# A spectral-mixer backward kernel: gelu products in the loaded tile, symmetric matrices without transposes, and gradient rows through a ring of three tiles

## Chip, cores, metric

One core of one Trainium2 chip. The metric is device time in microseconds (us) of one execution. Every run quoted here was in the fast state (granted TensorE clock 0.96 to 0.99 over the span); a trace is of one of these executions.

## The reference

A block with adaptive layer norm: a spectral filter (`rfft2`, product with a complex weight, `irfft2`), then an MLP with gelu. The kernel returns the output and all gradients, in bfloat16.

```python
# S = 2048 tokens, D = 1024, F = 3584
mod = (silu(c) @ w_mod).reshape(1, 6, 1, D)          # sa, ca, ga, sb, cb, gb
h = layernorm(x) * (1 + ca) + sa
x = x + ga * irfft2(rfft2(h) * (w_r + 1j * w_i))
h = layernorm(x) * (1 + cb) + sb
x = x + gb * (gelu(layernorm(h) @ w1 + b1) @ w2 + b2)
# outputs: x and the vjp for x, w_r, w_i, w1, b1, w2, b2, c, w_mod
```

## The kernel before

The transforms are products with cosine and sine matrices on TensorE. Three pieces of the program matter here; the cuts leave out hints to the scheduler.

(`tt` is a VectorE operation on two tensors.) The gelu block. The MLP runs over 28 of these (4 token blocks of 512, 7 groups of 512 features). Working tiles come in two sets, so block n+2 writes the tiles of block n. `ph` holds a product computed earlier (the gradient that comes back through w2), and `d_gz` takes the gradient that later stages read.

```python
zb, av, bv, sg, ph = gts[n % 2]
nc.sync.dma_start(out=ph, in_=d_ph_v[...])
for k in range(4):
    ...                                   # 8 matmuls into a bank pz
    nc.scalar.activation(out=zb[:, k, :], in_=pz[:], func=ACT.Identity, bias=...)   # evacuation, L767
nc.scalar.activation(out=av, in_=zb, func=ACT.Square)                               # L769
nc.vector.tensor_scalar(out=av, ...)
tt(bv, av, zb, ALU.mult)
nc.scalar.activation(out=sg, in_=bv, func=ACT.Sigmoid, ...)                         # L773
nc.scalar.activation(out=bv, in_=bv, func=ACT.Sigmoid, ...)
...                                       # more of the gelu on VectorE, result in av
for k in range(4):
    nc.vector.tensor_tensor_reduce(out=av[:, k, :], in0=ph[:, k, :], in1=av[:, k, :], ...)   # L784
nc.gpsimd.dma_start(out=d_gz_v[...], in_=av)                                        # L786
```

The spectral core, which runs forward and backward. It walks over eight pairs of frequency blocks; on the way it loads matrices transposed for the inverse transform.

```python
def load_smi(par):                        # par 0: even, par 1: odd matrices
    for t in range(2):
        for i in range(4):
            nc.sync.dma_start_transpose(out=smi[:, t, :, i * P:(i + 1) * P], in_=d_SF[:, par + 2 * t, i, :])
...
if par == 0 and m == 2:
    for cl in range(4):
        for h in range(2):
            nc.sync.dma_start_transpose(out=gm[...], in_=d_E[:, 0 if fwd else 1, 2 * cl + h, :])
```

The rows of the modulation weight's gradient, done beside the backward pairs: one step loads a tile of `w_mod`, scales the gradient row into an output tile, stores that, and reduces. There is one output tile (`gmy[:, 1:2]`) and one loaded tile.

```python
def gmod_steps(r, wrs, gws, gr):
    ...                                   # load the gradient row gr; wr, gw: this step's tiles
    for jc in range(NDC):
        nc.sync.dma_start(out=wr, in_=w_mod[...])
        nc.vector.tensor_scalar(out=gw, in0=gr, scalar1=u_rt[:, jc:jc + 1], ...)    # L899
        nc.gpsimd.dma_start(out=out_9[...], in_=gw)
        nc.vector.tensor_tensor_reduce(out=wr, in0=wr, in1=gr, ..., accum_out=gu[...])   # L901
        yield
```

TensorE fills the pairs with pieces of the w2 gradient (`gw2acc`), whose evacuation goes to `gwo` (two slots) and from there to memory by GpSimd.

## Time and profile before

| | before |
|---|---|
| median of the first three runs | 1582.85 us (1582.29 to 1590.55) |
| span of the traced run | 1578.6 us |
| TensorE idle in it | 128.9 us |
| gelu stage (first output product to first `pg`) | 427.4 us |
| backward spectral stage (first backward `pcs` to first `gw1acc`) | 225.7 us |

The windows view gives one stretch a line: length, then busy time of TensorE, weight loads, VectorE, ScalarE, GpSimd (instructions in brackets), granted clock, DMA share and GB/s. Kernel before: the gelu stage, the backward stage, and the part of the gelu stage where the idle time lies.

```profile
389.63:817.01 427.38, 390.05 (x1727) 170.80 (x1726) 295.35 (x435) 232.94 (x216) 79.07 (x84) 0.95 0.76 225
1131.98:1357.65 225.67, 194.69 (x945) 93.90 (x944) 136.66 (x196) 76.10 (x116) 59.12 (x67) 0.94 0.76 195
400.00:580.00 180.00, 153.15 (x661) 66.41 (x660) 138.63 (x213) 104.24 (x95) 32.43 (x34) 0.92 0.62 194
```

TensorE idles 37.3 and 31.0 us in these two stages, over half of its idle time. Two lines of the waits view (400 to 830 us and 385 to 830 us: what waits, for whom, total us, times, longest) tell who stands in front of it in the gelu stage, and the list of transfers how long the store takes to land (count, size, median us):

```profile
ACT gt L769 <- DMA d_gz<-gt: 58.1, 10, 14.0
SPq L758 <- DVE gb_acc L784: 143.7, 21, 20.7
d_gz<-gt POOLq DMA_DIRECT2D x28, 512.0 KB, 6.5
```

ScalarE waits at the square for the store of `av` to land. SyncE waits at the load of `ph` for the last product, which costs nothing as long as the load comes in time.

### The profile page before, as it was taken

The page shows a single profiled execution, that of the slowest core. Times are in us where ns is not written, and L with a number is a line of the kernel's source. Part 1 is how long each engine was busy: PE and PEld are TensorE (multiplying, and loading weights), DVE is VectorE, ACT ScalarE, POOL GpSimd, SP SyncE. Part 2 cuts the span into 40 slices and gives each one's busy share as a digit, 9 for nine tenths or more (in the row PEclk, how much of TensorE's full clock was granted, in tenths as well). Part 3 has the DMA queues.
Part 4 walks back from the last instruction along what each step waited for, and adds up shares of the span by engine and source line. Part 5 has one row for each costly group of instructions (what it writes and reads, how often), then busy time and mean ns, then how long its engine had stood idle before and what let it go on. Part 6 is the DMA issues. An engine that isn't in the chain of part 4 may idle for free.

```text
span 1578.6 us, 18397 instructions
## 1 busy us (share of the span) xinstructions
PE 1449.7 (92%) x6831; PEld 669.1 (42%) x6831; DVE 1074.5 (68%) x1578; ACT 722.3 (46%) x955; POOL 366.7 (23%) x427
## 2 busy tenths in 40 slices
PE   5989899999797989999899999989979869999998
PEld 2434454444343334444344444434434434444443
DVE  5992869887777787877323977976237556898733
ACT  4756556668565565665111423332522424442211
POOL 5710611101112122212111101312014421322423
PEclk8999999999999999999899999999999989999999
DMA  9961937998475766799955446496379857855996
GB/s 329 294 164 54 241 120 238 252 298 279 163 209 174 214 207 233 217 293 270 312 192 175 141 141 213 112 275 155 77 177 238 204 175 222 215 168 144 264 205 191
DMA packets 372514, 325.33 MB, mean 206 GB/s; under 512 B 224436, under 2 KB 315586, under 8 KB 372297
## 3 DMA queue, kind: packets, MB, share of 16 engines
q1 hardware_dynamic: 338680, 209.81, 51.4%
q0 software_dynamic: 33744, 114.36, 20.8%
q8 instruction: 53, 0.87, 0.2%
q14 instruction: 37, 0.30, 0.1%
HBM read 162.57 MB, written 108.05 MB: 171 GB/s over the span
## 4 chain that ended last, share of the span: by engine, by line
PE 39%; DVE 12%; DMA 7%; issue 6%; ACT 3%; SPq 1%; POOL 1%; POOLq 0%; ACTq 0%; DVEq 0%
PE gw1acc L1116 9%; PE gw2acc L1049 7%; PE pbo L805 7%; PE pg L956 5%; PE pz L764 5%; DVE got L882 2%; PE pu L450 2%; DVE gn3a L887 1%; DMA gB<-in_grad_out_dram 1%; DMA d_gz<-gt 1%; DMA gzh<-d_gz 1%; PE pv L543 1%; DVE gt L172 1%; DVE qb L172 1%; SPq L580 1%
## 5 line engine op out<-in xcount | busy, mean ns | idle before, releaser
L647 PE MATMUL pp<-gBoT,wt 128*128 128x512 bf16 x896 | 200.6, 379 | 2.8 <-DMA wt<-in_B_w_dram 1.9
L1116 PE MATMUL gw1acc<-gzh,n3n 128*128 128x512 bf16 x896 | 196.5, 379 | 1.2 <-DMA gzh<-d_gz 1.2
L956 PE MATMUL pg<-w1T,gzr 128*128 128x512 bf16 x896 | 196.7, 381 | 0.4 <-ACT gn3b L961 0.2
L764 PEld LDWEIGHTS <-w 128*128 128x128 bf16 x896 | 89.6, 100 | 140.7 <-issue 40.2
L956 PEld LDWEIGHTS <-gzr 128*128 128x128 bf16 x896 | 87.9, 98 | 107.9 <-issue 3.4
L1116 PEld LDWEIGHTS <-n3n 128*128 128x128 bf16 x896 | 87.6, 98 | 105.1 <-issue 1.5
L647 PEld LDWEIGHTS <-wt 128*128 128x128 bf16 x896 | 87.4, 98 | 104.9 <-DMA wt<-in_B_w_dram 2.4
L764 PE MATMUL pz<-n3Ta,w 128*128 128x512 bf16 x448 | 102.1, 388 | 16.6 <-ACT gt L767 16.6
L764 PE MATMUL pz<-n3Tb,w 128*128 128x512 bf16 x448 | 105.4, 395 | 11.0 <-ACT gt L767 7.7
L1049 PE MATMUL gw2acc<-gB,hhsA 128*128 128x512 bf16 x448 | 102.0, 384 | 0.0
L805 PEld LDWEIGHTS <-hhA 128*128 128x128 bf16 x608 | 60.1, 100 | 81.2 <-issue 13.7
L767 ACT ACTIVATE gt<-pz,b_col 128x512 bf16<-128x512 f32 x112 | 72.7, 682 | 39.7 <-PE pz L764 39.0
L1054 ACT CAST gwo<-gw2acc 128x512 bf16<-128x512 f32 x53 | 30.1, 583 | 129.5 <-PE gw2acc L1049 78.0
L769 ACT ACTIVATE gt<-gt 128x2048 bf16<-128x2048 bf16 x28 | 53.4, 1908 | 59.9 <-DMA d_gz<-gt 59.5
L1120 ACT CAST gwo<-gw1acc 128x512 bf16<-128x512 f32 x48 | 27.8, 583 | 111.1 <-PE gw1acc L1116 97.2
L172 DVE TENSOR_TENSOR gt<-gt,gt 128x2048 bf16<-128x2048 bf16 x56 | 68.2, 1222 | 14.4 <-ACT gt L775 13.5
L172 DVE TENSOR_TENSOR ct<-ct 128x2048 bf16<-128x2048 bf16 x64 | 76.0, 1219 | 1.3 <-DMA d_n<-ct 0.5
L773 ACT ACTIVATE gt<-gt 128x2048 bf16<-128x2048 bf16 x28 | 53.4, 1910 | 36.1 <-DVE gt L172 36.0
L1049 PEld LDWEIGHTS <-hhsA 128*128 128x128 bf16 x448 | 44.3, 99 | 51.9 <-issue 2.5
L1049 PE MATMUL gw2acc<-gB,hht 128*128 128x512 bf16 x256 | 57.9, 388 | 7.3 <-DVE gB L172 7.3
L1049 PE MATMUL gw2acc<-gB,otl 128*128 128x512 bf16 x192 | 45.5, 395 | 19.5 <-DVE gwo L1054 11.3
L543 PE MATMUL pv<-smi,R 128*128 128x512 bf16 x256 | 58.6, 384 | 4.0 <-DVE R L172 4.0
(306 smaller groups left out, 2538.6 us busy)
## 6 DMA issues: line engine op xcount, KB each, us to landing
d_gz<-gt POOLq DMA_DIRECT2D x28, 512.0 KB, 6.5
gzr<-d_gz SPq DMA_DIRECT2D x28, 512.0 KB, 4.9
wblk<-in_w_mod_dram SPq DMA_DIRECT2D x12, 1024.0 KB, 11.9
d_ph<-pho POOLq DMA_DIRECT2D x21, 512.0 KB, 5.1
out_dram<-otl POOLq DMA_DIRECT2D x40, 256.0 KB, 4.3
d_hh<-hhA POOLq DMA_DIRECT2D x19, 512.0 KB, 4.3
w2sD<-in_B_w_dram SPq DMA_DIRECT2D x14, 512.0 KB, 7.1
hhC<-d_ph SPq DMA_DIRECT2D x14, 512.0 KB, 5.1
```

The source lines that it names most:

```text
L172: return nc.vector.tensor_tensor(out=out, in0=a, in1=b, op=op)
L450: last_pu[0] = nc.tensor.matmul(pu[:], lhsT=fb[:, i, cl, c8 * P:(c8 + 1) * P], rhs=sm[:, i, :], start=(i == 0), stop=(i == 3))
L543: nc.tensor.matmul(pv[:], lhsT=R[:, cl * 4 + m, :, :].rearrange("p x w -> p (x w)")[:, base:base + 255:2], rhs=smi[:, cl // 2, m, :], star ...
L647: last_pe[0] = nc.tensor.matmul(pp[:], lhsT=wt[:, fg % 2, cch, k * P:(k + 1) * P], rhs=gBoT[j][:, cch, :], start=(cch == 0), stop=(cch == ...
L764: last_pe[0] = nc.tensor.matmul(pz[:], lhsT=w1s[g][:, cch, k * P:(k + 1) * P], rhs=n3T[:, cch, :], start=(cch == 0), stop=(cch == NDC - 1))
L767: nc.scalar.activation(out=zb[:, k, :], in_=pz[:], func=ACT.Identity, bias=b1_col[:, fc:fc + 1], scale=1.0)
L769: nc.scalar.activation(out=av, in_=zb, func=ACT.Square)
L773: nc.scalar.activation(out=sg, in_=bv, func=ACT.Sigmoid, scale=2.0 * GK)
L805: last_pe[0] = nc.tensor.matmul(pbs[i][:], lhsT=hh[:, k, i * P:(i + 1) * P], rhs=wp[:, k, :], start=False, stop=(g == 6 and k == 3))
L956: nc.tensor.matmul(pgs[i][:], lhsT=gzt[g][:, k, i * P:(i + 1) * P], rhs=w1Ts[g][:, k, h * KH:(h + 1) * KH], start=(g == 0 and k == 0), sto ...
L1049: nc.tensor.matmul(acc[:], lhsT=hh_s[hh_o[fc]][:, t, :], rhs=gBs[t // 4][:, t % 4, h * KH:(h + 1) * KH], start=(t == 0), stop=(t == NT - 1))
L1116: nc.tensor.matmul(acc[:], lhsT=n3ns[t // 4][:, t % 4, cch * P:(cch + 1) * P], rhs=gz2[t // 8][:, t % 8, :], start=(t == 0), stop=(t == NT ...
```

## The change

Intent: take the store out of the tile that ScalarE writes first in a later block; fewer of the transposed loads (one of `smi` or `gm` holds SyncE for about 1.25 us), since the odd matrices are symmetric and need none, and the even ones can be kept from the forward pass in a scratch tensor `d_SI`; modulation rows through three tiles, loaded two steps ahead, with the step's output written into the tile it loaded. A copy out of `pa` gets high priority. The core of it:

```diff
-                nc.vector.tensor_tensor_reduce(out=av[:, k, :], in0=ph[:, k, :], in1=av[:, k, :], ...)
+                nc.vector.tensor_tensor_reduce(out=ph[:, k, :], in0=ph[:, k, :], in1=av[:, k, :], ...)
-            nc.gpsimd.dma_start(out=d_gz_v[...], in_=av)
+            nc.gpsimd.dma_start(out=d_gz_v[...], in_=ph)
 # --- spectral core
-        def load_smi(par):
+        def load_smi():                       # even matrices alone
             for t in range(2):
-                for i in range(4):
-                    nc.sync.dma_start_transpose(out=smi[...], in_=d_SF[:, par + 2 * t, i, :])
+                if fwd:
+                    for i in range(4):
+                        nc.sync.dma_start_transpose(out=smi[...], in_=d_SF[:, 2 * t, i, :])
+                else:
+                    nc.sync.dma_start(out=smi[:, t], in_=d_SI[:, t])
+            if fwd:
+                nc.gpsimd.dma_start(out=d_SI[:], in_=smi[:])
+            smis.extend((smi, sms[1]))        # odd: the forward matrices themselves
 # gm: eight transposes at m == 2 become plain loads of CO and SO at m == 1
 #     and two transposes each for CE (m == 2) and SE (m == 3)
 # --- modulation rows
+    def gmod_ring(rows, bufs, gr):
+        load_g(rows[0]); load_w(0); load_w(1)
+        yield
+        for n, (r, jc) in enumerate(steps):
+            buf = bufs[n % 3]
+            nc.vector.tensor_tensor_reduce(out=buf, in0=buf, in1=gr, ..., accum_out=gu[:, r, jc:jc + 1])
+            nc.vector.tensor_scalar(out=buf, in0=gr, scalar1=u_rt[:, jc:jc + 1], ...)
+            nc.gpsimd.dma_start(out=out_9[...], in_=buf)
+            ...                               # load the next row if it changes
+            if n + 2 < len(steps):
+                load_w(n + 2)
+            yield
 # beside a pair: `if k < (0, 2, 2, ...)[n]` becomes `if 3 - k < (1, 2, 2, ...)[n]`,
 #     so its steps come after the last pieces of the w2 gradient, not after the first
 # --- output passes
-        if b == 0:
-            nc.vector.tensor_copy(out=gacc[:, cs_], in_=pa[0:1, :])
-        else: ...
+        with tc.high_priority():
+            if b == 0: ...
```

The ring serves row 5 (in the stage before) and rows 3 and 4 (beside the backward pairs). Rows 2, 1 and 0, at the end, keep the old routine.

More of the change, by code (lines that the diff above doesn't have):

```diff
@@ L112 @@
     d_SF = dram.tile([P, 4, 4, 512], BF16, name="d_SF")
+    d_SI = dram.tile([P, 2, 4, 512], BF16, name="d_SI")
     d_E = dram.tile([P, 2, 8, 256], BF16, name="d_E")
@@ L553, in spectral_core @@
         smis = []
-        def load_smi(par):
-            smi = reg.tile([P, 2, 4, 512], BF16, name="smi", tag=("sma", "smb")[par])
+        def load_smi():
+            smi = reg.tile([P, 2, 4, 512], BF16, name="smi", tag="sma")
             for t in range(2):
-                for i in range(4):
-                    with tc.issue_after(ld_in[0].ins):
-                        nc.sync.dma_start_transpose(out=smi[:, t, :, i * P:(i + 1) * P], in_=d_SF[:, par + 2 * t, i, :])
-            smis.append(smi)
+                with tc.issue_after(ld_in[0].ins):
+                    if fwd:
+                        for i in range(4):
+                            nc.sync.dma_start_transpose(out=smi[:, t, :, i * P:(i + 1) * P], in_=d_SF[:, 2 * t, i, :])
+                    else:
[3 more added lines that the diff above has]
+            smis.extend((smi, sms[1]))
         pair_load(0)
@@ L572, in spectral_core @@
                 beside(par * 4 + m)
-                if par == 0 and m < 2:
-                    load_smi(m)
-                if par == 0 and m == 2:
-                    gm = reg.tile([P, 12, 256], BF16, name="gm", tag="gm")
-                    for cl in range(4):
+                if par == 0 and m == 0:
+                    load_smi()
+                if par == 0 and m > 0:
+                    v = 0 if fwd else 1
+                    if m == 1:
+                        gm = reg.tile([P, 12, 256], BF16, name="gm", tag="gm")
+                        for cl in (CO, SO):
+                            with tc.issue_after(ld_in[0].ins):
+                                nc.sync.dma_start(out=gm[:, 2 * cl:2 * cl + 2, :], in_=d_E[:, v, 2 * cl:2 * cl + 2, :])
+                    else:
+                        cl = (CE, SE)[m - 2]
                         for h in range(2):
@@ L580, in spectral_core @@
                                 nc.sync.dma_start_transpose(out=gm[:, 2 * cl:2 * cl + 2, h * P:(h + 1) * P],
-                                                            in_=d_E[:, 0 if fwd else 1, 2 * cl + h, :])
+                                                            in_=d_E[:, v, 2 * cl + h, :])
         s_inv(CO, smis[1])
@@ L783, in z_block @@
                 fc = g * 4 + k
-                nc.vector.tensor_tensor_reduce(out=av[:, k, :], in0=ph[:, k, :], in1=av[:, k, :], scale=1.0, scalar=0.0,
+                nc.vector.tensor_tensor_reduce(out=ph[:, k, :], in0=ph[:, k, :], in1=av[:, k, :], scale=1.0, scalar=0.0,
                                                op0=ALU.mult, op1=ALU.add, accum_out=gb1_acc[:, fc, b:b + 1])
-            nc.gpsimd.dma_start(out=d_gz_v[:, g * 4:(g + 1) * 4, b * BW:(b + 1) * BW], in_=av)
+            nc.gpsimd.dma_start(out=d_gz_v[:, g * 4:(g + 1) * 4, b * BW:(b + 1) * BW], in_=ph)
     w2_v = B_w2.rearrange("(c p) d -> p c d", p=P)
@@ L824, in bo_pass @@
                 last_pe[0] = nc.tensor.matmul(pa[:], lhsT=ones_bf[:], rhs=go[:, i, :], start=(i == 0), stop=(i == 3))
-        if b == 0:
-            nc.vector.tensor_copy(out=gacc[:, cs_], in_=pa[0:1, :])
-        else:
-            tt(gacc[:, cs_], gacc[:, cs_], pa[0:1, :], ALU.add)
+        with tc.high_priority():
+            if b == 0:
+                nc.vector.tensor_copy(out=gacc[:, cs_], in_=pa[0:1, :])
+            else:
+                tt(gacc[:, cs_], gacc[:, cs_], pa[0:1, :], ALU.add)
     def bo_both(b):
@@ L903, in gmod_steps, with load_w, load_g @@
             yield
+    def gmod_ring(rows, bufs, gr):
+        steps = [(r, jc) for r in rows for jc in range(NDC)]
+        def load_w(n):
+            r, jc = steps[n]
+            nc.sync.dma_start(out=bufs[n % 3], in_=w_mod[jc * P:(jc + 1) * P, r * D:(r + 1) * D])
+        def load_g(r):
+            nc.sync.dma_start(out=gr, in_=d_gmod[r * D:(r + 1) * D].partition_broadcast(P))
+        load_g(rows[0])
+        load_w(0)
+        load_w(1)
+        yield
+        for n, (r, jc) in enumerate(steps):
+            buf = bufs[n % 3]
+            nc.vector.tensor_tensor_reduce(out=buf, in0=buf, in1=gr, scale=1.0, scalar=0.0,
+                                           op0=ALU.mult, op1=ALU.add, accum_out=gu[:, r, jc:jc + 1])
+            nc.vector.tensor_scalar(out=buf, in0=gr, scalar1=u_rt[:, jc:jc + 1], scalar2=None, op0=ALU.mult)
+            nc.gpsimd.dma_start(out=out_9[jc * P:(jc + 1) * P, r * D:(r + 1) * D], in_=buf)
+            if n + 1 < len(steps) and steps[n + 1][0] != r:
+                load_g(steps[n + 1][0])
+            if n + 2 < len(steps):
+                load_w(n + 2)
+            yield
     w1Ts = []
@@ L922 @@
     gmg = reg.tile([P, 2, D], BF16, name="gmg", tag="sb")
-    early = gmod_steps(5, gmw[:], gmg[:, 0:1], gmg[:, 1, :])
+    early = gmod_ring((5,), [gmw[:, 0], gmw[:, 1], gmg[:, 0]], gmg[:, 1, :])
+    next(early)
     au = reg.tile([P, 4, D], BF16, name="au", tag="px1")
@@ L966 @@
             ln_bwd(gn3[:, i, :], sums[:, 0, i:i + 1], n3u[:, i, :], stats[:, 2, 0, t:t + 1], gn3[:, i, :], got[:, 4 + i % 2, :])
+        next(early, None)
         tt(pru, gn3[:], n2u[:], ALU.mult)
@@ L978 @@
             ln_bwd(g2[:, i, :], s2c[:, i:i + 1], n2u[:, i, :], stats[:, 1, 0, t:t + 1], g2[:, i, :], got[:, 4 + i % 2, :])
+        next(early, None)
         tt(g2[:], g2[:], go4, ALU.add)
@@ L987 @@
             sums3_ga(b, au)
-            for _ in range(3):
-                next(early, None)
+            next(early, None)
     hhp = reg.tile([P, 2, NT, P], BF16, name="hhsA", tag="px1")
@@ L1006 @@
     pfs = [empf[:, 2048:2048 + 4 * PW].rearrange("p (s r w) -> p s r w", s=2, r=2), pf1[:]]
-    otl = reg.tile([P, 2 * NT * P + D], BF16, name="otl", tag="ot")
+    otl = reg.tile([P, 2 * NT * P + 2 * D], BF16, name="otl", tag="ot")
     hht = [reg.tile([P, 2, NT, P], BF16, name=f"hht{k}", tag=f"t{k + 2}") for k in range(2)]
-    gmy = otl[:, NT * P:2 * NT * P].rearrange("p (a d) -> p a d", d=D)
+    gmy = [otl[:, NT * P + k * D:NT * P + (k + 1) * D] for k in (0, 1, 3)]
     sacc = otl[:, 2 * NT * P:2 * NT * P + D]
@@ L1147, in mid_bwd @@
             nc.sync.dma_start(out=d_gmod[r * D:(r + 1) * D].rearrange("(o n) -> o n", o=1), in_=rows[32 * k:32 * k + 1, :])
-    rows34 = [gmod_steps(r, gmy[:, 0:1], gmy[:, 1:2], sacc) for r in (3, 4)]
-    side = [0]
+    rows34 = gmod_ring((3, 4), gmy, sacc)
     def beside_bwd(n):
@@ L1154, in beside_bwd @@
             fill(1)
-            if k < (0, 2, 2, 2, 2, 2, 3, 3)[n]:
+            if 3 - k < (1, 2, 2, 2, 2, 2, 3, 3)[n]:
                 with tc.issue_after(hh_in[0].ins):
-                    next(rows34[side[0] // NDC])
-                side[0] += 1
+                    next(rows34)
     spectral_core(False, fbuf2, (smA2, smB2), em2, [css2[:, 0], css2[:, 1]],
```

## The prediction

> **What bounds the kernel now.** I read the page's busy line first, then the busy time per 20 us stretch, then TensorE's waits split by stage, then the timeline around each long wait.
>
> ```profile
> PE 1449.7 (92%) x6831; PEld 669.1 (42%) x6831; DVE 1074.5 (68%) x1578; ACT 722.3 (46%) x955; POOL 366.7 (23%) x427
> ```
>
> TensorE is the bound: it works 1449.7 of 1578.6 us. No part of the change removes a matmul (the order of instructions shows 13664 TensorE rows before and after, half of them weight loads), so the change can win only out of the 129 us in which TensorE is idle, plus slow matmuls that follow an idle spell. Of those 129 us, some 25 are start-up (the first 100 us) and some 7 the last 40 us; neither is touched. Two stages hold most of the rest: the gelu stage (400 to 580 us: 26.9 us idle) and the backward spectral stage (1160 to 1300 us: 30.5 us idle). TensorE's waits in each:
>
> ```profile
> PE pz L764 <- ACT gt L767: 23.2, 4, 8.2
> PE pbo L805 <- DMA w2sC<-in_B_w_dram: 4.1, 1, 4.1
> PE pa L824 <- DVE otile L172: 3.3, 1, 3.3
> PE pz L764 <- DVE w2sD L826: 3.2, 1, 3.2
> ```
>
> ```profile
> PE pcs L483 <- ACT cs01b L613: 11.4, 8, 4.4
> PE gw2acc L1049 <- DVE gwo L1054: 11.3, 1, 11.3
> PE gw2acc L1049 <- DMA otl<-d_hh: 8.2, 1, 8.2
> ```
>
> The first list is 400 to 830 us, the second 1100 to 1310 us. Columns: total us, times, longest. In 90 to 400 us no wait of TensorE is over 4 us, and only one, of 1.9 us, is for a DMA that SyncE issued.
>
> The releaser named is only the last link, so I followed the longest wait of the gelu stage back through the timeline:
>
> ```profile
> 406.56 0.75 POOL L786 DMA_DIRECT2D d_gz<-gt  x1 [9.54 <-DVE gb_acc L784]
> 413.90 1.91 ACT L769 ACTIVATE gt<-gt 128x2048 bf16<-128x2048 bf16 x1 [11.70 <-DMA d_gz<-gt]
> 422.80 2.40 ACT L767 ACTIVATE gt<-pz,b_col 128x512 bf16<-128x512 f32 x4
> 423.52 8.68 PE L764 MATMUL pz<-n3Ta,w 128*128 128x512 bf16 x32 [8.22 <-ACT gt L767]
> ```
>
> The square of block n+2 (L769) writes the tile from which the store d_gz of block n still reads. ScalarE stands until the store has landed, the PSUM evacuations (L767) stand behind it in ScalarE's order, and TensorE runs out of banks. ScalarE waits 58.1 us in 10 times for this store in the stage.
>
> The backward stage has two such knots. SyncE issues eight transposes of gm in a row, and the transposed load that TensorE needs stands behind them; later VectorE works off modulation rows one at a time because their single output buffer must be stored first, and a PSUM evacuation (L1054) stands behind those:
>
> ```profile
> 1165.40 11.97 SPq L580 DMA_TRANSPOSE gm<-d_E  x8
> 1177.47 2.10 SPq L1074 DMA_TRANSPOSE otl<-d_hh  x1
> 1181.85 8.41 PE L1049 MATMUL gw2acc<-gB,otl 128*128 128x512 bf16 x32 [8.18 <-DMA otl<-d_hh]
> ...
> 1281.82 0.48 DVE L899 TENSOR_SCALAR otl<-otl,u_rt 128x1024 bf16<-128x1024 bf16 x1 [2.68 <-DMA out_dram<-otl]
> 1285.00 0.48 DVE L899 TENSOR_SCALAR otl<-otl,u_rt 128x1024 bf16<-128x1024 bf16 x1 [2.70 <-DMA out_dram<-otl]
> 1289.01 0.69 DVE L1054 CAST gwo<-gw2acc 128x512 bf16<-128x512 f32 x1
> 1289.75 0.58 PE L1049 MATMUL gw2acc<-gB,otl 128*128 128x512 bf16 x1 [11.31 <-DVE gwo L1054]
> ```
>
> **What the Trainium skill says.** (1) "TensorE: Matmul & The Clock Gate", section What's actually happening: after an idle window of about 3.4 us the array runs at half clock, until it has been busy about as long. The trace agrees: 32 warm matmuls take 6.91 us (216 ns each), the 8 after the wait of 7.21 us at 566.77 us take 3.55 us (444 ns each). So each long wait costs more than its own length. (2) "Perfetto Trace Analysis", section What "DMA-bound" means: an issuing engine whose track is solid DMA slices is itself the limit, and the slices are descriptor generation. The trace agrees: SyncE is solid for 11.97 us over eight transposes, and one smi transpose holds it 1.265 us (median of 32). (3) "DMA: Bandwidth & Descriptors", section Two DMAs through the same engine are not ordered: only the completion semaphore says that a buffer is free. So each ring slot and each reused tile costs a whole landing: 6.5 us median for d_gz, 4.3 us for a modulation store out of otl. No page prices these stalls themselves.
>
> **The change part by part.**
>
> *Gelu products into the loaded tile.* The products and the store d_gz move from the working tile av to ph. VectorE does the same work. ScalarE's L769 no longer waits for a store, only for the last product. The four waits of TensorE behind L767: at 423.5 (8.2 us) L769 could start at 406.3 and not 413.9, so about 7.5 come back; at 497.7 (4.3) L769 starts 12 us earlier, all back; at 523.7 (3.4) 8 us earlier, all back; at 566.8 (7.2) 7 us earlier, but VectorE is nearly solid there, so about 6. Sum 21.2. The copy of pa at high priority removes the 3.2. Half-clock matmuls after these five, each run against 216 ns per matmul: 1.8 + 1.9 + 2.9 + 1.8 + 1.6 = 10.0. Ceiling 34.4 us. Against it: VectorE is busy 138.6 of the 180 us; if the stage shrank by 34 it would be 95% busy, with chains between it and ScalarE. I take it to stop near 89%, a stage of 156 us: **gain 24 us**.
>
> *Price of that part.* The next load of ph now waits for the store that reads it, and SyncE waits with it. Block n: products done, store 6.5, load 5.1, so about 12 us, against some 23 until block n+2 needs the tile (two blocks of 32 matmuls of 216 ns each, plus 1.4 output passes of 3.45 us per block). It fits. Loads of w2 queued behind may come 6 or 7 us late; they have four slots.
>
> *Symmetric odd matrices.* Transposes of smi go from 32 to 8 and of gm from 16 to 8; 6 plain loads and one store of 1 MB come in. SyncE's issue time saved: 24 x 1.265 + 8 x 1.244 = 40.3 us, less 6 x about 0.45. Forward almost nothing of it is on the path. Backward the run of eight gm transposes becomes 2 + 2 transposes and 2 plain loads, spread over three pairs, and the smi transposes are gone: the 8.2 us wait goes, and with it 1.5 us of slow matmuls.
>
> *Ring of three.* The same 16 steps over the eight pairs, but the order of instructions shows VectorE now doing two (once three) modulation steps after each pair's own work, where before ten half-steps (seven scalings, three reductions) stand in a row ahead of the seventh pair. Loads come two steps ahead; before, VectorE waited 30.6 us for them and 24.2 us for the stores in this stage. The 11.3 us wait and the 3.2 and 2.2 us after and before it should go for the most part; the 4.4 us one stems from ScalarE waiting for the gwo store behind GpSimd's row stores (9.95 us at 1228.6), and GpSimd's order there is little better. Slow matmuls after these: 2.9 at 1230, 3.3 at 1290. Ceiling for the backward stage: 11.4 + 11.3 + 8.2 + 1.5 + 2.9 + 3.3 = 38.6 us. I keep about two thirds: **gain 25 us**.
>
> *Elsewhere.* The rows in the n3 stage sit beside matmuls that are 97% busy (860 to 1020 us): 0. The last 270 us keep the old routine for rows 2, 1, 0: 0.
>
> Sum: 24 + 25, less 6 us kept for new waits that I can't place (late w2 loads, ring loads that hold SyncE until a store has landed) = 43. 1582.85 - 43 = 1540 us.
>
> **Rivals.**
> *A, VectorE becomes the bound of the gelu stage.* For: 77% busy over 400 to 580 us, and in 544 to 572 us almost without a gap. Against: from 580 to 740 us the same blocks run with TensorE at 100% and VectorE near 76%. It would leave 12 of the 24 us: about 1552 us.
> *B, SyncE takes the place of the removed wait.* It issues in order, and now holds at ph loads for a landed store and at ring loads for the store one step back. For: it already waited 144.6 us at the ph loads, and in the backward stage the stores of GpSimd it waits for stand behind others. Against: the sums above leave about 10 us of slack, and the removed transposes give it 40 us. It would cost up to 20 us: about 1560 us.
> *C, nearly all waits go.* 34 + 39 us: about 1512 us.
> *D, nothing:* the gaps reappear later because one DMA path feeds all. DMA is at 1.0 share only for parts of the span (660 to 800 us), so I give it little: 1575 us.
>
> **Range and chances.** The main line gives 1540; A and B alone land at the 2% line (1551) or beyond it, and together at about 1570; C gives the lower end. Range 1520 to 1563. Faster by over 2% 0.70, within 2% 0.28, slower 0.02.
>
> **What would show it.** Right: ScalarE's wait at the square for d_gz gone from 58 us to near 0; TensorE idle in 400 to 580 us down from 27 to under 10 us; SyncE waiting for d_gz at the ph loads instead; the waits of TensorE for otl and gwo in the backward stage under 10 us in sum; matmul busy time down by some 10 us, as fewer run at half clock. Wrong: TensorE waiting for w2 or hhsA loads (B), or again for L767 while VectorE shows over 90% (A), or for pcs as before (ring worth less than thought).

## The result

1522.28 us median (1517.34 to 1526.08, 4 runs), against 1584.53 for the kernel before in the same session (1582.29 to 1590.55, 4 runs). The ratio is 0.960, 95% interval 0.956 to 0.964: faster. A ratio is the mean time of one kernel's fast runs over that of the other's of the same rounds, so not quite the ratio of the medians quoted. The outputs agree with the reference.

The span of the traced run fell from 1578.6 to 1521.4 us, by 57.2. Below, lines of the changed kernel's profile: the page's line for TensorE; then the windows view, the same two stages and nearly the same work as in 400 to 580 us of before (653 of 661 matmuls).

```profile
PE 1437.8 (95%) x6831; PEld 667.6 (44%) x6831; DVE 1072.0 (70%) x1577; ACT 722.1 (47%) x956; POOL 363.5 (24%) x428
```

```profile
388.75:779.83 391.08, 379.47 (x1727) 168.59 (x1727) 293.10 (x435) 231.50 (x215) 75.67 (x84) 0.99 0.84 246
1096.99:1299.33 202.34, 190.71 (x945) 92.64 (x944) 136.17 (x195) 76.33 (x117) 59.08 (x67) 0.99 0.83 211
400.00:544.00 144.00, 141.44 (x653) 63.36 (x652) 134.29 (x210) 100.51 (x91) 30.06 (x34) 1.00 0.76 224
```

The gelu stage gained 36.3 us, the backward stage 23.3; the other four stretches of the span lost 2.4 in sum. TensorE's busy time fell by 11.9 us with the same 6831 matmuls: fewer of them ran at half clock. In the gelu stage TensorE's idle time fell from 37.3 to 11.6 us and its busy time by 10.6. In 144 us VectorE now does nearly the work that took 180 (134.3 us against 138.6): it is 93% busy there.

The waits view in 385 to 830 us (TensorE, ScalarE, SyncE); L776 is L764 of before, L779 is L767, L781 is L769, L770 is L758:

```profile
PE pbo L817 <- DMA w2sC<-in_B_w_dram: 1.9, 1, 1.9
PE pz L776 <- ACT gt L779: 1.3, 2, 1.1
ACT gt L781 <- DVE gb_acc L796: 6.9, 4, 4.2
SPq L770 <- DMA d_gz<-w2sA: 74.2, 11, 11.9
SPq L770 <- DMA d_gz<-hhC: 71.7, 12, 13.5
```

The square waits for the last product (6.9 us) and for no store. TensorE's wait behind the evacuations went from 23.2 us (24.3 if one counts from 385 us here too) to 1.3. SyncE waits as long as before, 145.9 us against 143.7, only for the landed store where it was for the product. The timeline at the place of the first long wait:

```profile
404.55 1.91 ACT L781 ACTIVATE gt<-gt 128x2048 bf16<-128x2048 bf16 x1 [4.16 <-DVE gb_acc L796]
404.75 0.76 POOL L798 DMA_DIRECT2D d_gz<-w2sA  x1 [9.51 <-DVE gb_acc L796]
408.48 0.37 SPq L770 DMA_DIRECT2D w2sA<-d_ph  x1
```

The square starts beside the store, and not 7 us after it; the load of `ph` (here named for its place, w2sA) follows 3.7 us after the store's issue. In the backward stage TensorE's waits are now these (1097 to 1300 us):

```profile
PE pcs L484 <- ACT cs01b L625: 8.3, 8, 3.0
PE gw2acc L1090 <- DMA otl<-d_hh: 2.0, 1, 2.0
```

The waits for `gwo` (11.3) and for `otl` (8.2) are gone or down to 2.0; the eight short ones for `pcs` stay.

### The profile page after: what moved, and what is told of

It is laid out like the page before. It is cut to its first block, busy times and chain, and to the rows that moved or that the text cites. A ratio compares the mean times of both kernels' runs of the same rounds, so it can differ in the third digit from the quotient of the medians.

```text
span 1521.4 us, 18355 instructions
## 1 busy us (share of the span) xinstructions
PE 1437.8 (95%) x6831; PEld 667.6 (44%) x6831; DVE 1072.0 (70%) x1577; ACT 722.1 (47%) x956; POOL 363.5 (24%) x428
## 4 chain that ended last, share of the span: by engine, by line
PE 47%; DVE 22%; DMA 10%; issue 10%; ACT 6%; POOL 3%; SPq 1%; POOLq 0%; ACTq 0%; DVEq 0%
PE pbo L817 11%; PE pz L776 9%; PE gw2acc L1090 8%; PE pg L996 5%; DVE ct L173 4%; PE pv L544 3%; PE pu L451 3%; PE gw1acc L1157 2%; PE pp L659 2%; DVE got L895 2%; DVE fbuf L173 1%; DMA gB<-in_grad_out_dram 1%; DVE gn3a L900 1%; DMA out_dram<-otl 1%; DVE gt L173 1%
## 5 line engine op out<-in xcount | busy, mean ns | idle before, releaser
L776 PEld LDWEIGHTS <-w 128*128 128x128 bf16 x896 | 87.7, 98 | 109.0 <-issue 3.8
L776 PE MATMUL pz<-n3Tb,w 128*128 128x512 bf16 x448 | 99.1, 379 | 1.5 <-DVE w2sD L839 1.5
L776 PE MATMUL pz<-n3Ta,w 128*128 128x512 bf16 x448 | 98.7, 379 | 1.3 <-ACT gt L779 1.3
L779 ACT ACTIVATE gt<-pz,b_col 128x512 bf16<-128x512 f32 x112 | 72.9, 684 | 29.5 <-PE pz L776 29.0
L785 ACT ACTIVATE gt<-gt 128x2048 bf16<-128x2048 bf16 x28 | 53.4, 1910 | 64.4 <-DVE gt L173 64.4
L781 ACT ACTIVATE gt<-gt 128x2048 bf16<-128x2048 bf16 x28 | 53.5, 1910 | 7.6 <-DVE gb_acc L796 6.9
L787 ACT ACTIVATE gt<-gt 128x2048 bf16<-128x2048 bf16 x28 | 53.3, 1909 | 0.4
L1162 POOL DMA_DIRECT2D out_dram<-gwo x56 | 30.7, 551 | 77.9 <-ACT gwo L1161 38.3
## 6 DMA issues: line engine op xcount, KB each, us to landing
wblk<-in_w_mod_dram SPq DMA_DIRECT2D x12, 1024.0 KB, 13.4
```

The costliest lines, as they stand in the source:

```text
L776: last_pe[0] = nc.tensor.matmul(pz[:], lhsT=w1s[g][:, cch, k * P:(k + 1) * P], rhs=n3T[:, cch, :], start=(cch == 0), stop=(cch == NDC - 1))
L785: nc.scalar.activation(out=sg, in_=bv, func=ACT.Sigmoid, scale=2.0 * GK)
L787: nc.scalar.activation(out=bv, in_=bv, func=ACT.Sigmoid, scale=-2.0 * GK)
```

## The experiments

In three batches and one last run (e12), each timed against the kernel before on the same chip; for e12, 11 of the 12 runs of before are those of the third batch. The lengths of the two stages in the traced runs say more than the sums, so here they are for all (the stages are cut at the same matmuls in each; us):

| kernel | gelu stage | backward stage | span | ratio to before, 95% interval |
|---|---|---|---|---|
| before | 427.4 | 225.7 | 1578.6 | 1 |
| changed | 391.1 | 202.3 | 1521.4 | 0.960 (0.956 to 0.964) |
| e1 before + products in `ph` | 391.0 | 223.5 | 1544.4 | 0.978 (0.975 to 0.982) |
| e2 changed, products in `av` | 420.8 | 205.8 | 1551.2 | 0.985 (0.982 to 0.988) |
| e3 before + products in `sg` | 399.0 | 226.9 | 1550.4 | 0.983 (0.980 to 0.986) |
| e3b before + products in `zb` | 427.4 | 225.3 | 1589.1 | 1.007 (1.003 to 1.010) |
| e4 before + symmetric matrices | 427.7 | 212.3 | 1567.3 | 0.995 (0.993 to 0.996) |
| e5 changed, transposes back | 388.5 | 219.0 | 1535.2 | 0.975 (0.973 to 0.977) |
| e6 before + ring | 425.5 | 212.0 | 1568.8 | 0.996 (0.993 to 0.998) |
| e7 changed, old row routine | 388.2 | 214.8 | 1533.7 | 0.972 (0.970 to 0.973) |
| e8 changed + extra VectorE work | 393.0 | 201.7 | 1521.4 | 0.967 (0.963 to 0.971) |
| e9 changed, `gwo` stored by ScalarE | 389.3 | 213.8 | 1527.1 | 0.965 (0.961 to 0.969) |
| e10 changed, first groups interleaved | 389.0 | 209.7 | 1526.8 | 0.963 (0.960 to 0.967) |
| e12 changed, indirect stores later | 385.3 | 211.9 | 1523.8 | 0.973 (0.969 to 0.976) |

Kernels with the same gelu code differ by up to 6 us there (385.3 to 391.1), and with the same backward code by up to 7 (e6 and e5, 212.0 and 219.0), since each edit moves the schedule elsewhere; differences below that are not read. The records of e8 to e10 and e12 lack about a hundred matmuls, so TensorE's busy time is not compared for these.

### e1: the products alone

```diff
-  tensor_tensor_reduce(out=av[:, k, :], in0=ph[:, k, :], in1=av[:, k, :], ...)
+  tensor_tensor_reduce(out=ph[:, k, :], in0=ph[:, k, :], in1=av[:, k, :], ...)
-  nc.gpsimd.dma_start(out=d_gz_v[...], in_=av)
+  nc.gpsimd.dma_start(out=d_gz_v[...], in_=ph)
```

> The kernel before with one edit: the four products of a gelu block and the store of d_gz use the loaded tile ph in place of the working tile. Theory (the gelu stage gained because the square of block n+2 no longer waits for the store of block n to land): nearly the whole gain of that stage comes with this edit alone, -28 to -36 us, so 1547 to 1556 us; ScalarE's wait at the square for d_gz falls from 58 us to 0; VectorE over 90% busy in the gelu stage; the backward stage keeps its 30 us of idle time. Rival 1 (the stage gained from the shorter queue of transposes on SyncE or from the copy of pa at high priority): under 8 us of gain. Rival 2 (my prediction's size, VectorE stops the stage at about 89% busy): -24 us, 1559.

Measured: 1547.35 us (1542.79 to 1550.54, 4 runs). The windows view for its gelu stage:

```profile
391.62:782.64 391.02, 379.24 (x1726) 168.68 (x1726) 292.20 (x434) 232.86 (x215) 78.17 (x84) 0.99 0.82 246
```

The whole gain of the gelu stage (391.0 against 391.1 in the changed kernel) comes with this edit, without the copy of `pa` at high priority and without a transpose less. The wait for the store is gone (first line, ScalarE at the square, 385 to 830 us), and the backward stage keeps its wait for `gwo` (second line) and its waits for `otl` (8.7 us in two). Rivals 1 and 2 fall.

```profile
ACT gt L769 <- DVE gb_acc L784: 6.8, 4, 4.1
PE gw2acc L1049 <- DVE gwo L1054: 12.0, 1, 12.0
```

### e2: the products taken back

The same two lines undone in the changed kernel.

> The changed kernel with that one edit undone: products and store in the working tile again. Theory: the gelu stage goes back to some 424 us, so +28 to +36 us, 1550 to 1558 us, with ScalarE again waiting 50 us or more for d_gz at the square, while the backward stage keeps its gain. Rival (other parts would have brought the gain anyway): under 8 us above the changed kernel.

Measured: 1556.22 us (1553.01 to 1560.69, 4 runs); the stage is 29.7 us longer than in the changed kernel, and ScalarE's waits are back:

```profile
ACT gt L781 <- DMA d_gz<-gt: 59.0, 12, 12.0
```

The backward stage keeps its gain. The stage is 6.6 us shorter than before, at the limit of what is read; the priority of the `pa` copy may be in it, but between e1 and the changed kernel it makes no difference.

### e3 and e3b: the same store, other tiles

If waiting for the landing is the price, it must depend on when the tile is next written, and on nothing else of it. In e3 products and store use `sg`, written 3.9 us after the square begins; in e3b `zb`, written by the evacuations ahead of it.

```diff
-  tensor_tensor_reduce(out=av[:, k, :], ...)  ;  dma_start(out=d_gz_v[...], in_=av)
+  tensor_tensor_reduce(out=sg[:, k, :], ...)  ;  dma_start(out=d_gz_v[...], in_=sg)     # e3; zb in e3b
```

> The kernel before with the products and the store in another working tile, sg, which ScalarE writes again 3.9 us after it begins the square (square 1.9, two VectorE instructions 0.7 and 1.2). The store lands as late as before, only the first overwriting is 3.9 us later. Theory (waiting for the landing is the whole price): the ten waits of 58.1 us in sum shrink by up to 3.9 us each and move to the sigmoid, so between a third and two thirds of the gain of the products in ph: -10 to -24 us, 1559 to 1573 us. Rival (it is the loaded tile itself that helps, by delaying the ph loads and so easing the DMA): no gain, 1578 to 1588 us.

> The kernel before with the products and the store in zb, the tile that the PSUM evacuations of block n+2 write, some 7 us earlier than the square's output. Theory: the evacuations themselves wait for the landing, TensorE's banks stay full longer, each wait grows by up to 7 us: slower than before by 15 to 60 us, 1598 to 1643 us. Rival (position of the wait doesn't matter): within 8 us of before.

Measured: e3 1552.91 us (1551.84 to 1558.32, 4 runs), e3b 1591.76 us (1588.14 to 1594.47, 4 runs). The waits view in 385 to 830 us, first e3, then e3b:

```profile
ACT gt L773 <- DMA d_gz<-gt: 10.5, 4, 4.4
```

```profile
ACT gt L767 <- DMA d_gz<-gt: 45.9, 14, 10.0
PE pz L764 <- ACT gt L767: 33.7, 7, 9.5
```

In the totals the order is as the theory wants it: `zb` worst, then `av`, `sg`, `ph`, with the wait at the instruction that writes the tile. In the gelu stage by itself `zb` and `av` are alike (427.4 us). The sizes were off. In e3 the stage gained 28.4 of 36.3 us, more than the 24 that I expected at most: ten waits less 3.9 us each are 39 of 58.1 us, and the measured fall is from 58.1 (59.5 from 385 us) to 10.5. The 3.9 us were the least distance: in the trace of e3 the sigmoid begins 3.9 us or more after the square in all but one of the 28 blocks, 5.0 in the median and up to 7.6, as VectorE's two instructions wait their turn. In e3b I expected at least 15 us; the whole kernel is 10 us slower, 8 of these ahead of the first output product (at 397.3 us, before at 389.6), as ScalarE's waits at the evacuations (45.9 us) replace those at the square and do not come on top. The loaded tile as such is not what helps.

### e4 and e5: the symmetric matrices alone, and all but these

> The kernel before with the symmetric matrices alone (24 smi and 8 gm transposes fewer). Theory: only the 8.2 us wait for otl behind the run of eight gm transposes and the 1.5 us of slow matmuls after it are on the path: -7 to -10 us, 1573 to 1576 us; forward nothing. Rival (another wait, for gwo or pcs, takes its place within the same pair): 0 to -3 us.

> The changed kernel with the transposes back. Theory: +7 to +10 us, 1529 to 1532 us, a wait of TensorE for otl or hhsA of 6 us or more at the gm transposes. Rival (with the ring in place SyncE has the room for them): 0 to +3 us.

(The edit is the spectral-core part of the diff above, alone in e4, undone in e5.) Measured: e4 1570.95 us (1568.56 to 1573.29, 6 runs), e5 1540.39 us (1537.05 to 1541.83, 5 runs). TensorE's waits in the backward stage, e4 and then e5:

```profile
PE gw2acc L1061 <- DVE gwo L1066: 12.2, 1, 12.2
PE pcs L484 <- ACT cs01b L625: 6.6, 8, 3.2
```

```profile
PE pcs L483 <- ACT cs01b L613: 11.8, 8, 3.0
PE gw2acc L1078 <- DMA otl<-d_hh: 6.1, 1, 6.1
```

With the transposes gone no long wait for `otl` is left (none in e4, 2.0 us in the changed kernel), and with them it is there, with and without the ring: that link is shown. The stage shows 13.4 us (e4) and 16.7 us (e5), where my working has 9.7; the differences of 3.7 and 7.0 us are not above what kernels with the same backward code show. In these two pairs the `pcs` waits shrink too (11.4 to 6.6 us in e4, and 8.3 in the changed kernel against 11.8 in e5), but e1 and e3, which keep the transposes, have 8.3 and 8.7 us of them, so it is not shown that the transposes stretch them. In total e4 came out as expected (9 us by medians), e5 higher (14 us over the changed kernel by the spans, more by the medians, which are of different sessions). In e4 2.6 us were lost again in the stretch just ahead of that stage, where TensorE waits for `gB` (8.1 us, 7.3 before). Whether the `smi` or the `gm` transposes matter more was not tested: both experiments move them together.

### e6 and e7: the ring alone, and all but the ring

> The kernel before with the ring of three tiles alone, for row 5 and for rows 3 and 4. Theory: the 11.3 us wait for gwo behind the row of ten half-steps goes, with the 5 us around it and 3.3 us of slow matmuls; the pcs waits stay: -12 to -18 us, 1566 to 1572 us. Rival (SyncE, held by ring loads ahead of gm's eight transposes, makes new waits for hhsA or otl): -5 us or less.

> The changed kernel with the old routine for the modulation rows. Theory: +12 to +18 us, 1534 to 1540 us, VectorE again with many half-steps in a row and a wait for gwo of 8 us or more. Rival (the symmetric matrices gave VectorE its room, the ring is worth little): under +5 us.

(The edit is the modulation-row part of the diff, alone in e6, undone in e7.) Measured: e6 1573.35 us (1565.74 to 1576.72, 6 runs), e7 1535.50 us (1532.13 to 1536.49, 5 runs). TensorE's longest wait in the backward stage, e6 and then e7:

```profile
PE pcs L483 <- ACT cs01b L613: 9.1, 8, 2.5
```

```profile
PE gw2acc L1062 <- DVE gwo L1067: 11.9, 1, 11.9
```

The 11 to 13 us wait for `gwo` is in every kernel with the old routine (before, e1, e3, e3b, e4, e7) and in none with the ring (e2, e5, e6, the changed one and those made from it). The stage shows 13.7 us (e6) and 12.5 us (e7). In e6 the gain in total is smaller than expected, some 7 us by the ratio and 9.8 by the spans; 3.3 us were lost ahead of the stage and 1.7 in the first stretch. Each part is worth some 13 us alone and both together 23.3. Whether they overlap cannot be read: added alone they sum to 27.1 us, taken out of the changed kernel to 29.2, and e6 and e5 differ by 7.0 with the same backward code. Nor is the ring split up: its third tile, the earlier loads, the order of reduction and scaling and the place of the steps beside a pair were changed together.

### e8: more work for VectorE in the gelu stage

```diff
             tt(hh, sg, zb, ALU.mult)
+            tt(hh, sg, zb, ALU.mult)      # same product again, 28 times
```

> The changed kernel with one VectorE product of every gelu block done twice (hh = sg * zb, same output, 28 instructions of 1.22 us, 34 us of VectorE in all). In 400 to 544 us VectorE works 134.3 of 144 us, so 9.7 us are free, and some 11 to 12 of the 28 blocks lie there (13 to 15 us more work). If VectorE is now just under being the bound of that stretch, the excess of 3 to 5 us at least must show, and with the chain to ScalarE more: +4 to +15 us, 1526 to 1537 us. If VectorE still has room in the sense of my prediction's rival (it stops the stage at about 89% busy), the stage would grow by the whole 13 to 15 us or more. If there is slack in other blocks to absorb it: under +3 us.

Measured: 1528.35 us (1523.03 to 1534.92, 6 runs). Windows view of the same stretch as in the result:

```profile
400.00:544.00 144.00, 139.96 (x629) 62.63 (x641) 140.34 (x211) 99.54 (x91) 31.14 (x33) 0.99 0.71 226
```

VectorE is 97% busy here and did 27.9 us more in the stage, yet the stage is 393.0 us, 1.9 longer, which is too little to be read, and the span the same. The traced run is one of the two fastest of six: the median is 6 us above that of the changed kernel, which was measured in another session, and by the ratio e8 is 0.7% (11 us) slower. So a price between 0 and 11 us stays open, and with it whether VectorE is just under being the bound or has slack elsewhere. Either way VectorE does not stop this stage at 89% or at 93%.

### e9, e10, e12: three attempts at what is left

```diff
-  nc.gpsimd.dma_start(out=out_6[...], in_=gwo[:, fc % 2])          # e9
+  nc.scalar.dma_start(out=out_6[...], in_=gwo[:, fc % 2])
-  for fc in (0, 1): for h in range(2): one bank, tokens 0 to 15    # e10
+  four banks (fc, h) at once, tokens 0 to 3, then 4 to 7, ...      # needs the fourth gB tile later
-  indirect stores of out_2, out_3 right after the pair             # e12
+  the same, issued after the second gwo store of that pair
```

> The changed kernel with the stores of gwo issued by ScalarE, which writes gwo, and not by GpSimd, where they stand behind indirect stores that wait for SyncE's plain stores. Theory (the 8.3 us of pcs waits left in the backward stage come from ScalarE waiting 42.3 us for these stores): ScalarE's wait for gwo's store falls below 15 us, the pcs waits below 3 us: -4 to -8 us against the changed kernel, 1514 to 1518 us. Rival (ScalarE pays for the issue, or the two slots of gwo are short anyway): 0 or slower.

> The changed kernel with the first four output groups of the gw2 product run token quarter by token quarter over four PSUM banks, so that the last of the four gB tiles is needed 10 us later. Theory (the wait of 8.4 us for gB at the start of that stage, and 2 to 4 us of half-clock matmuls after it, are paid because each group needs all four tiles at once): -5 to -9 us, 1513 to 1517 us. Rival (the stage then waits for its fold and the spectral product instead): 0 to -2 us.

> The changed kernel with the two indirect stores of each backward pair (which wait for SyncE's plain stores to the same output) issued after the second gwo store of that pair, and not between its first and its second; GpSimd stays the issuer of all. Theory (what is left in the backward stage comes from gwo's stores standing behind these indirect stores): ScalarE's wait for gwo's store falls from 42.3 us to under 15 us, the pcs waits from 8.3 us to under 3 us, the stage from 202.3 to 195 to 199 us: -3 to -7 us against the changed kernel. Rival (as with the issue from ScalarE, the freed time turns into another wait, here SyncE's loads of pf or GpSimd's loads of ws for the pair after next): stage within 3 us of 202.3 or longer.

Measured: e9 1525.86 us (1519.29 to 1532.38, 6 runs), e10 1524.24 us (1518.87 to 1528.97, 6 runs), e12 1537.45 us (1525.97 to 1541.54, 7 runs). None is faster than the changed kernel; e12 is slower (its interval lies above that of the changed kernel). The trace of e12 is of its fastest run, 11 us under its median, so it does not show all of the loss. TensorE's and SyncE's waits, one fence each for e9 (backward stage), e10 (start of the w2 gradient) and e12 (backward stage):

```profile
PE pv L544 <- DVE V L622: 13.3, 1, 13.3
```

```profile
PE gw2acc L1090 <- DMA hht<-d_hh: 9.0, 1, 9.0
```

```profile
PE gw2acc L1097 <- DMA hhsA<-d_hh: 8.2, 2, 5.4
SPq L473 <- DMA out_dram<-pf,xu: 26.4, 3, 9.5
```

e9 and e10 took away what they aimed at and got another wait for it; e12 did not. In e9 the `pcs` waits fell from 8.3 to 1.5 us, so that GpSimd issues these stores did cause most of them; but ScalarE now stood ahead of its own store for up to 8.7 us at a time (the trace names a load of `otl` as what ended that wait), and one evacuation of `pv` fell to VectorE, behind modulation steps that waited for their loads. In e10 the wait of 8.4 us for `gB` became one of 9.0 for the second load of `hht`, which interleaving needs earlier. In e12 SyncE waits for the later indirect stores before it reloads `pf` (26.4 + 19.5 us, where it was 30.0), and the transposed loads behind it come late; ScalarE's wait for `gwo`'s store did not even fall (55.9 us, was 42.3), so the theory of e12 is not confirmed, and what of GpSimd's work stands in front of these stores is not shown. The rest of the backward stage's idle time stays open.

## Why the prediction was right, and where a size was off

*What bounds the kernel, and where the gain can come from:* right. TensorE's matmuls stayed; its idle time fell from 128.9 to 83.6 us, and its busy time by 11.9 (predicted: some 10).

*The gelu mechanism:* right, shown by e1 to e3b. Of the waits that I summed, the ones behind the evacuations went (23.2 to 1.3 us). That the high priority of the `pa` copy removes the 3.2 us is not borne out: that wait only halved (1.5), it is 1.6 in e3b without the priority and 8.6 in e2 with it, and in e1, without it, the stage was as short. The section that I cited of the Trainium skill for the landing ("DMA: Bandwidth & Descriptors", Two DMAs through the same engine are not ordered) speaks of one DMA behind another; that an engine which writes the tile waits for the landing too is what this trace shows (58.1 us).

*The gelu size:* this is the step that failed, "I take it to stop near 89%": gain 24 us. The stage gained 36.3: TensorE's idle time there fell by 25.7 us (my sum of waits was 24.4) and its busy time by 10.6 (mine 10.0), so the ceiling of 34.4 was the right forecast and the cap the error. A 4.1 us wait for a load of w2, left out of the ceiling, fell to 1.9. VectorE went to 93%, and in the traced run of e8 to 97% with the stage longer by no more than can be read. A share of 77% averaged over a stage with the waits in it tells how much work there is, not how dense it can be packed: the same instructions fitted once nothing else stood in the chain. Rival A rested on the same cap and falls with it. Two slips beside it: in 544 to 572 us VectorE was not "almost without a gap" but busy for 23.3 of 28 us, and rival C's sum, 34 + 39 us off 1583, gives 1510 and not 1512.

*The price, SyncE's hold at the `ph` loads:* right that it fits. SyncE's wait is the same 145 us, and TensorE's waits for w2 are no longer than before. Rival B is not seen in the gelu stage; something like it is seen in e12.

*The backward stage:* gain predicted 25, measured 23.3, and both waits shown to go with their parts (e4 to e7). Term by term it is 11.3 us from `gwo`, 6.2 from `otl`, 3.1 from `pcs` and 4.0 from faster matmuls, less a new wait of 1.3 for `pv`. The "two thirds" of a ceiling was a judgement without a working, so that the sum came so close is in part luck. The symmetric matrices look undersized (9.7 against 13.4 and 16.7), at the limit of what can be read. That most of the `pcs` waits would stay held (8.3 us; e9 points to GpSimd as the issuer of the `gwo` stores, e12 does not confirm the order of its stores).

*The reserve of 6 us for new waits:* the other stretches gave back 2.4. With the gelu term at its measured size the sum would have been 36 + 25 - 6 = 55, near the measured 57 of the traced spans (62 by the medians of the session); rival C (1512), which let nearly all waits go, was closer to the measured 1522 than the main line (1540).

## What to carry to other kernels

When a store reads a working tile, ask which engine writes that tile next and how soon: the choice of tile alone, with no more memory, was worth 28 to 36 us here. An in-order engine that waits takes the innocent instructions behind it along, so the removal of a wait is worth its own length plus the half-clock matmuls after it; but when one more wait is attacked in a schedule this full, look first for the next thing the freed engine would stand for. And cap a gain by a busy engine only with a reason for the number: at 93% VectorE was no cap here, and whether 97% costs something stayed open.

## What the Trainium skill lacked or had wrong

- "DMA: Bandwidth & Descriptors", section Anatomy of one DMA, gives about 2.0 us plus bytes over 436 GB/s for one transfer, so by estimate 3.2 us for the 512 KB of a `d_gz` store. The trace of the changed kernel has for these stores 3.3 us at the least, 4.7 in the median and 9.9 at the most (before: 3.6, 6.5 and 8.4): here the fit is the floor, and a wait for a landing has to be sized from the trace.
- "Perfetto Trace Analysis", section Optimization Strategy, says that consistent bubbles "can mean there isn't enough SBUF/PSUM for the next tile to be allocated". In e3 the number and size of tiles stayed and only the tile that the store reads was another; 28.4 of 36.3 us came back. The page lacks this case, a wait that depends on which of a block's tiles is stored from.
- "DMA: Bandwidth & Descriptors", section Issuing engines are not separate DMA queues, tells that another issuer saves only the issue time. It lacks what an issuer in order costs or saves beside that: in e9, with the same transfers, TensorE's `pcs` waits went from 8.3 to 1.5 us, and a wait of 13.3 us came up elsewhere.
- No page tells how busy an engine off the matmul path can be before it holds the others up. Here VectorE at 93% did not; at 97% the traced stage was 1.9 us longer in 391, too little to be read, and the whole kernel between 0 and 11 us slower.
